# The ones beside the values, written by VectorE in place of ScalarE, in the opening of an attention and feed-forward block

**Chip, cores, metric.** One Trainium2 chip, one of its cores. The metric is device time in microseconds (us) of one execution; smaller is better.

## The reference, cut to what matters

A layer norm, attention of 32 heads of 16 features over 2048 positions, and a gated feed-forward layer, in bf16, with two residual additions:

```python
x = A_x                                            # 1 x 2048 x 512
h = x + attention(layernorm(x), A_wqkv, A_wo)      # 32 heads, head size 16, softmax over 2048 keys
n = layernorm(h)
return h + (sigmoid(n @ B_w_gate) * (n @ B_w_up)) @ B_w_down     # 512 -> 1792 -> 512
```

The softmax's sums come out of the same matmul as its weighted values: each head's 16 value columns have a 17th column of equal constants beside them. These are "the ones" (they hold 0.5). They are needed only when the first values are multiplied, after the first exponential.

## The kernel before: the parts concerned

`Vaug` holds the values: 128 partitions, 16 tiles x 32 heads x 17 columns of bf16. The ones are its last column: 512 elements in each partition, each 17 elements = 34 bytes from the next. The opening, in program order (each engine executes its own instructions in this order):

```python
Vaug = const.tile([P, NT, H, VW], BF16)            # NT=16, H=32, VW=17, DH=16
...
for i in range(TQ):                                # x tiles 0 to 3, two queues in turn
    load_x(0, i, 1, (nc.sync, nc.scalar)[i % 2])
...
nc.vector.memset(eps_t[:], 1e-5)
nc.scalar.activation(out=A0[:], in_=eps_t[:], func=ACT.Sqrt)     # loads the root's table early
fill = prep.tile([P, QC], BF16, name="fill")
nc.scalar.activation(out=Vaug[:, :, :, DH:VW], in_=eps_t[:].to_broadcast([P, NT * H]).rearrange(
    "p (t h o) -> p t h o", t=NT, o=1), func=ACT.Copy, scale=0.0, bias=0.5)      # the ones
nc.gpsimd.memset(fill[:], 1.0)                     # operand of TensorE's warming matmuls
nc.gpsimd.memset(eps4_t[:], 4e-5)
nc.gpsimd.memset(power[:], -0.5)
ramp = prep.tile([P, 2, 32], BF16, name="ramp")
for k in range(32):                                # 32 small memsets: 0, 1, ... 31
    nc.gpsimd.memset(ramp[:, 0, k:k + 1], float(k))
nc.gpsimd.tensor_scalar(out=eps4_t[:], in0=eps4_t[:], scalar1=1.0, scalar2=None, op0=ALU.mult)
...
nc.vector.memset(ident_bf[:], 0.0)
nc.vector.transpose(out=ramp[:, 1, :], in_=ramp[:, 0, :])        # waits for the ramp
for b in range(0, P, 32):                          # the identity: ramp == transposed ramp
    nc.vector.tensor_tensor(out=ident_bf[b:b + 32, b:b + 32], in0=ramp[b:b + 32, 0, :],
                            in1=ramp[b:b + 32, 1, :], op=ALU.is_equal)
...                                                # masks from the identity, on VectorE
```

Behind it the first layer norm runs from a fixed list. "As1" is the statistics of x tile 1 on ScalarE, "Ds0" those of tile 0 on VectorE, "Aq0" a root on ScalarE, "Dr0" a reciprocal and "Da0" a normalising on VectorE, "Pt0" a transposition on TensorE, "Pp10" a projection:

```python
START = "As1 Ds0 Ds2 Aq0 Dr0 Da0 Pt0 Aq2 Df1 Ds3 Aq1 Ae0 Pp10 Dr2 Da2 Aq3 Aexps ...".split()
```

So ScalarE reaches its statistics of tile 1 only after the ones, and VectorE takes two statistics (tiles 0 and 2) before the first reciprocal. TensorE executes matmuls on `fill` where it would be idle, so that its clock stays up.

## Time and profile before

| | before |
|---|---|
| device time, median of 3 runs | 732.0 us (731.65 to 732.0) |
| span of the profiled execution | 729.3 us |
| writing the ones (ScalarE, 512 elements per partition) | 2.36 us, from 3.04 us |
| VectorE's hole before the ramp's transpose | 1.45 us, 0.96 to 2.41 us |
| first reciprocal (VectorE) | 6.88 us |
| first transposition of a tile (TensorE) | 7.55 us |
| first exponential (ScalarE) | 12.68 us |

Positions are counted from the start of the profiled execution. The first exponential is the end of the opening: from there ScalarE is full to the end of the body. The lines of the profile behind the writing, the hole and the reciprocal are in the prediction. The one behind the first exponential, from the timeline (its columns are explained under the result), is:

```profile
12.68 3.77 ACT L1447 ACTIVATE pt<-PS 128x1024 f16<-128x1024 f32 x4 [0.50 <-PE PS L1067]
```

### The profile page before, as it was taken

What the parts mean: (1) busy time and instruction counts of PE and PEld (TensorE: products, weight loads), DVE (VectorE), ACT (ScalarE), POOL (GpSimd) and SP (SyncE); (2) the same over time, 40 slices, a digit from 0 to 9 for tenths busy, and PEclk for the clock granted to TensorE, in tenths of its full rate; (3) what the DMA queues carried; (4) which work ended last, traced back from release to release, by engine and by line L of the source; (5) the groups of instructions that cost most, each with busy time, mean ns of one, the idle gap of its engine ahead of it and who ended that gap; (6) DMA issues with size and microseconds to landing.
All of it is one profiled execution on the core that took longest, in us unless ns stands there. A gap on an engine that the chain in (4) does not pass through costs nothing.

```text
span 729.3 us, 26553 instructions
## 1 busy us (share of the span) xinstructions
PE 712.6 (98%) x11169; PEld 335.7 (46%) x11169; DVE 664.1 (91%) x1299; ACT 702.0 (96%) x787; POOL 426.4 (58%) x728
## 2 busy tenths in 40 slices
PE   8999999999999999999999999999999999999997
PEld 3322224444454445544545454545554455445564
DVE  7989989999999998999999999989999999999952
ACT  8999999999999999999999999999999999999962
POOL 2725657775566755656656766566664665666610
PEclk9999999999999999999999999999999999999999
DMA  8300006000223013211224023301322133013450
GB/s 259 88 11 10 11 8 178 2 3 2 74 78 95 14 33 105 85 45 46 67 62 109 9 82 89 75 17 44 106 67 60 39 103 103 10 24 89 117 161 19
DMA packets 85741, 47.39 MB, mean 65 GB/s; under 512 B 17520, under 2 KB 85616, under 8 KB 85616
## 3 DMA queue, kind: packets, MB, share of 16 engines
q1 hardware_dynamic: 85328, 45.37, 22.1%
q8 instruction: 89, 1.46, 0.9%
q14 instruction: 36, 0.29, 0.1%
q10 hardware_dynamic: 288, 0.26, 0.1%
HBM read 37.75 MB, written 2.10 MB: 55 GB/s over the span
## 4 chain that ended last, share of the span: by engine, by line
PE 69%; ACT 20%; DVE 7%; issue 2%; DMA 1%; POOL 1%; SPq 0%; ACTq 0%; DVEq 0%; POOLq 0%
PE PS L1067 23%; PE PS L1235 20%; ACT pt L1447 13%; PE PS L803 12%; PE PS L821 6%; DVE J L1259 3%; PE PS L321 3%; ACT xnT L1447 2%; PE PS L326 2%; PE PS L746 2%; ACT xb L1447 1%; ACT th L833 1%; ACT QTb L1447 1%; POOL J L1280 1%; DMA out_dram<-ob 1%
## 5 line engine op out<-in xcount | busy, mean ns | idle before, releaser
L1280 POOL INT64_ADD J<-J x658 | 407.9, 632 | 253.5 <-DVE J L1259 207.2
L1447 ACT ACTIVATE pt<-PS 128x1024 f16<-128x1024 f32 (+2 forms) x523 | 519.9, 1117 | 2.9 <-PE PS L1067 2.4
L1259 DVE TENSOR_SCALAR J<-PS 128x512 int16<-128x512 f32 x626 | 411.5, 678 | 17.7 <-PE PS L1067 12.6
L1067 PE MATMUL PS<-QT,KT 32*128 32x256 bf16 (+1 forms) x3712 | 264.1, 276 | 8.6 <-ACT pt L1447 3.6
L1235 PE MATMUL PS<-J,Vaug 128*17 128x256 f16 (+1 forms) x3195 | 226.1, 279 | 0.5 <-DVE J L1304 0.3
L1235 PE MATMUL PS<-pt,Vaug 128*17 128x256 f16 (+1 forms) x2042 | 198.3, 279 | 0.0
L1067 PEld LDWEIGHTS <-KT 32*128 32x128 bf16 x3840 | 89.7, 92 | 204.3 <-issue 200.5
L1235 PEld LDWEIGHTS <-Vaug 128*17 128x17 bf16 x5841 | 131.5, 90 | 78.4 <-issue 73.6
L803 PE MATMUL PS<-xnT,wgu 128*128 128x256 bf16 x784 | 112.9, 275 | 0.0
L1447 ACT ACTIVATE xnT<-PS 128x1024 f16<-128x1024 f32 (+1 forms) x85 | 92.2, 1116 | 0.5 <-PE PS L1067 0.2
L1304 DVE TENSOR_TENSOR J<-J 128x1024 f16<-128x1024 f16 (+1 forms) x110 | 78.4, 713 | 12.7 <-POOL J L1280 12.2
L803 PEld LDWEIGHTS <-wgu 128*128 128x128 bf16 x784 | 63.8, 98 | 38.5 <-issue 32.7
L821 PE MATMUL PS<-wd,hT 128*128 128x512 bf16 x196 | 56.7, 384 | 0.0
L833 ACT ACTIVATE th<-PS 128x512 f32<-128x512 f32 (+1 forms) x63 | 38.8, 616 | 8.8 <-DVE hT L816 5.0
L1235 PE MATMUL PS<-xnT,Vaug 128*17 128x256 f16 x346 | 46.7, 274 | 0.0
L1447 ACT ACTIVATE QTb<-PS 128x1024 f16<-128x1024 f32 x40 | 44.0, 1100 | 0.0
L875 DVE SCALAR_TENSOR_TENSOR hT<-th,PS 128x512 bf16<-128x512 f32 x49 | 33.1, 676 | 0.8 <-PE PS L803 0.8
L1134 DVE STREAM_TRANSPOSE xs<-PS 128x256 f32<-128x256 f32 (+1 forms) x60 | 27.5, 458 | 1.7 <-PE PS L1235 1.4
L1105 DVE TENSOR_TENSOR o<-xs,rsum 128x128 bf16<-128x128 f32 (+1 forms) x60 | 24.5, 409 | 2.1
L1447 ACT ACTIVATE xb<-PS 128x1024 f16<-128x1024 f32 (+1 forms) x25 | 26.0, 1086 | 0.3 <-issue 0.2
L1235 PE MATMUL PS<-QTb,Vaug 128*17 128x256 f16 x160 | 25.7, 274 | 0.0
L1447 ACT ACTIVATE pe<-PS 128x1024 f16<-128x1024 f32 (+1 forms) x21 | 21.9, 1094 | 0.9 <-PE PS L1067 0.8
(126 smaller groups left out, 390.7 us busy)
## 6 DMA issues: line engine op xcount, KB each, us to landing
wgu<-in_B_w_gate_dram SPq DMA_DIRECT2D x49, 256.0 KB, 3.0
wgu<-in_B_w_up_dram SPq DMA_DIRECT2D x49, 256.0 KB, 3.4
out_dram<-ob SPq DMA_DIRECT2D x16, 128.0 KB, 1.7
QT<-qd SPq DMA_DIRECT2D x112, 16.0 KB, 1.8
wd<-in_B_w_down_dram SPq DMA_DIRECT2D x1, 1792.0 KB, 9.2
xr<-in_A_x_dram SPq DMA_DIRECT2D x14, 128.0 KB, 3.4
xb<-in_A_x_dram SPq DMA_DIRECT2D x6, 256.0 KB, 5.5
J<-in_B_w_gate_dram SPq DMA_DIRECT2D x4, 384.0 KB, 4.3
```

The costliest lines, as they stand in the source:

```text
L803: nc.tensor.matmul(ps[:, 0:PARTS[r][2]].rearrange("p (i q) -> p i q", q=P), lhsT=w[:, d, :], rhs=hn_of(r)[:, :, d, :], start=(d == 0), sto ...
L821: nc.tensor.matmul(ps, lhsT=hT[:, f, i * P:(i + 1) * P], rhs=wd[:, f, :], start=(f == 0), stop=(f == FC - 1))
L833: nc.scalar.activation(out=th[:, 0:ps.shape[-1]], in_=ps, func=ACT.Tanh, scale=0.5)
L875: nc.vector.scalar_tensor_tensor(out=hT[:, f:f + k, 0:w], in0=th[f][:].rearrange("p (k n) -> p k n", k=k), scalar=1.0, in1=ps2.rearrange(" ...
L1067: nc.tensor.matmul(pss[:, ui, i * CW[qc]:(i + 1) * CW[qc]], lhsT=KT[g // 2][32 * j:32 * j + 32, k * P:(k + 1) * P], rhs=q[32 * j:32 * j + ...
L1105: nc.vector.tensor_tensor(out=o2[:, 0:w // 32, DH * a:DH * a + DH], in0=xs[:, 0:w // 32, 0:DH], in1=rec.to_broadcast([P, w // 32, DH]), op ...
L1134: j = dve(650 - ns[0], lambda: nc.vector.transpose(out=xs[:, 0:w // 32, :].rearrange("p b r -> p (b r)"), in_=src), LAST, st["xs"], pr=-1)
L1235: nc.tensor.matmul(dst[32 * j:32 * j + VW, 0:w], lhsT=un.v[:, kt * SPAN[qc] + i, h, :], rhs=un.ap[:, i * w:(i + 1) * w], start=clears and ...
L1259: nc.vector.tensor_scalar(out=J[:, 0, k, :], in0=src, scalar1=ZOFF, scalar2=float(-min(CHORDS)), op0=ALU.add, op1=ALU.max)
L1280: nc.gpsimd.int64_add(words(s), words(0), CHORDS[s - 1] * (1 + 2 ** 16 + 2 ** 32 + 2 ** 48))
L1304: nc.vector.tensor_tensor(out=f1, in0=f1, in1=J[:, 0, 0:k, :].bitcast(FP16), op=ALU.add)
L1447: ex = nc.scalar.activation(out=pt, in_=pss[:, 0:wa, :], func=ACT.Exp, scale=AS)
```

## The change

Intent: VectorE waits 1.45 us for the ramp anyway. Let it write the ones there, "in single-rate mode", and so take 2.36 us from ScalarE, which is on the path to the first exponential.

```diff
     fill = prep.tile([P, QC], BF16, name="fill")
-    nc.scalar.activation(out=Vaug[:, :, :, DH:VW], in_=eps_t[:].to_broadcast([P, NT * H]).rearrange(
-        "p (t h o) -> p t h o", t=NT, o=1), func=ACT.Copy, scale=0.0, bias=0.5)
     nc.gpsimd.memset(fill[:], 1.0)
...
     nc.vector.memset(ident_bf[:], 0.0)
+    nc.vector.tensor_scalar(out=Vaug[:, :, :, DH:VW], in0=eps_t[:].to_broadcast([P, NT * H]).rearrange(
+        "p (t h o) -> p t h o", t=NT, o=1), scalar1=0.0, scalar2=0.5, op0=ALU.mult, op1=ALU.add)
     nc.vector.transpose(out=ramp[:, 1, :], in_=ramp[:, 0, :])
```

Nothing else changes its place on any engine.

## The prediction

> **What bounds the kernel now.** I read the page of the kernel before from the top: busy times, then the slices, then the chain that ended last.
>
> ```profile
> span 729.3 us, 26553 instructions
> PE 712.6 (98%) x11169; PEld 335.7 (46%) x11169; DVE 664.1 (91%) x1299; ACT 702.0 (96%) x787; POOL 426.4 (58%) x728
> PE 69%; ACT 20%; DVE 7%; issue 2%; DMA 1%; POOL 1%; SPq 0%; ACTq 0%; DVEq 0%; POOLq 0%
> ```
>
> TensorE and ScalarE are both busy nearly to the end, and the page's slices show no hole anywhere. In the body, from 13 us to about 697 us, ScalarE runs its exponentials end to end (the busy table by stretch gives 17.00 of 17.00 us from 13 to 30 us and 239.27 of 240.00 us from 240 to 480 us). So a microsecond saved before the first exponential moves the whole body earlier by about a microsecond, unless a later wait swallows it. A microsecond is 0.14% of the span, so the question is not whether 2% is reached but how much of the opening shrinks. Therefore I went to the opening: the first 13 us in the timeline of single instructions, and the chain of work that ended last over the same stretch.
>
> The chain, in order of time (start, length, what):
>
> ```profile
> 1.64 1.28 ACT L251
> 2.92 0.01 issue
> 2.93 0.20 ACT warm L251
> 3.13 2.26 ACT Vaug L253
> 5.40 0.52 ACT junk L364 x2
> 5.92 0.02 issue
> 5.94 0.72 ACT junk L366 x2
> 6.66 0.19 ACT QT L381
> 6.86 0.02 issue
> 6.88 0.17 DVE QT L418
> ```
>
> The instruction that the change removes, the writing of the ones (L253), is on the chain with 2.26 us. Behind it on ScalarE stand the statistics of x tile 1 (L364, L366) and the first square root (L381), and VectorE waits 1.40 us for that root before its reciprocal (L418), on which the normalising, transposing and projecting of the first tiles depend.
>
> VectorE's rows in the same timeline show the hole that the change wants to use:
>
> ```profile
> 0.80 0.06 DVE L250 MEMSET eps_t<- 128x1 f32 x1 [0.80 <-PEq L1665]
> 0.85 0.11 DVE L265 MEMSET ident_bf<- 128x64 uint32 x1
> 2.41 0.21 DVE L266 STREAM_TRANSPOSE ramp<-ramp 128x32 bf16<-128x32 bf16 x1 [1.45 <-POOL ramp L260]
> 2.65 0.70 DVE L268 TENSOR_TENSOR ident_bf<-ramp 32x32 bf16<-32x32 bf16 x4
> 3.39 0.29 DVE L272 TENSOR_REDUCE mask<-ident_bf 128x2 f32<-128x128 bf16 x1
> 3.71 0.17 DVE L274 TENSOR_SCALAR maskz<-mask 128x2 f32<-128x2 f32 x1
> 3.79 0.69 DVE L281 BATCH_NORM_STATS2 st<-xb 128x6 f32<-128x512 bf16 x1
> ```
>
> The hole is 1.45 us long, from 0.96 to 2.41 us, and ends when GpSimd has written the ramp (32 small memsets, 1.25 to 2.37 us). From 2.41 us to 5.48 us VectorE has no hole at all, so whatever sticks out beyond 2.41 us delays everything after it on VectorE one for one.
>
> **What the Trainium skill says.** "ScalarE: Activation LUTs", section "What ACT_TABLE_LOAD costs", gives an ACTIVATE with immediate scale and bias 186 ns + 0.833 ns per element: 186 + 512 x 0.833 = 612 ns. The trace agrees for the zeroing of an accumulator from the same broadcast source (L430, 128x512, contiguous, into PSUM: 607 ns) and disagrees with L253 (2357 ns). Source and count are the same; what differs is the destination, single bf16 elements 17 elements (34 bytes) apart in SBUF. "SBUF — State Buffer", section "Door 1: The DMA port swizzle", names a reason: SBUF has 16-byte cachelines and an access that crosses to a new line pays. That fits the extra (2357 - 607) / 512 = 3.4 ns per element, though this trace alone does not show it. "Vector Engine (DVE) Microarchitecture Reference", section 5.2 "Measured stream behaviour on trn2", has the same for VectorE: a destination that steps 24 words at each element ran at 2.50 ns per element instead of 1.05. "Advanced Engine Details and Errata", section "VectorE Performance Modes", says that a two-port mode takes SBUF source and destination with even outer counts, and that its second port is shared with GpSimd, so that the two block each other. The trace has a two-port rate at fp32 in its tail (L1623, 128x512: 419 ns, against 678 ns for the PSUM-sourced L1259), and the same-shaped normalising at L791 ranges from 514 to 828 ns beside a busy GpSimd, which would fit such blocking.
>
> **The change part by part.**
>
> Removed: one ACTIVATE of ScalarE, 2.36 us in its row, 2.26 us of it on the chain. Not all comes back, because the statistics need x tile 1. That tile's load is issued at 0.73 us and lands 2.8 us later, at 3.5 us. They can then start at about 3.55 us. The two passes take 0.54 + 0.18 + 0.03 + 0.72 = 1.47 us, where 0.54 us is the gap from L366 to its accumulator read, taken for both passes since the first was held back by L253's tail. They end at 5.02 us, the root 0.19 us later at 5.21 us, in place of 6.86 us: 1.65 us earlier. Now VectorE is the later one: the statistics of tile 2 occupy it until 5.48 us, and the reciprocal starts at about 5.39 us (back-to-back instructions overlap by some 0.09 us) in place of 6.88 us: 1.49 us earlier. The normalised tile 0 is then ready at about 6.0 us in place of 7.5 us.
>
> The next limit is TensorE's static order: 13 warming matmuls run from 1.31 to 6.44 us whatever happens. The first transpose comes after them, at 6.35 to 6.45 us in place of 7.55 us: 1.1 to 1.2 us earlier. From there each step has room: the first copy of a transposed tile on ScalarE ends at about 7.4 us (8.57), after four more warming matmuls the first projection starts at about 7.5 us (8.65); its weights, issued at 1.67 us with 4.35 us to land, are there at 6.05 us, the others at 6.55 us. On ScalarE the fourth root follows the copy, then the exponential's table load, at about 7.6 us (8.93). On VectorE the remaining normalising keeps its 1.49 us. The last transpose, copy and projection before the first scores come out 1.1 to 1.3 us earlier, and so does the first exponential, 12.68 us before. The value weights are issued at 3.80 us and take 5.7 us, so 9.5 us is early enough for their first use, now near 12.2 us.
>
> Added: one tensor-scalar of VectorE on 512 strided elements. The instruction order of the two builds confirms that it stands between the zeroing of the identity and the ramp's transpose, that the other engines keep their orders, and that no engine gets a new wait for it; it only waits for VectorE's own first memset. It can start at 0.98 us. Its length is the open term. In single-rate mode without a stride penalty it would take about 0.68 us (as the other 512-element single-rate instructions here); with the skill's strided 2.50 ns per element, an estimate, 512 x 2.50 = 1.28 us plus about 0.1 us fixed = 1.4 us, ending at 2.4 us, just inside the hole; with ScalarE's own per-element cost, 4.24 ns, 2.2 to 2.3 us, ending at 3.25 us.
>
> Nothing else moves: the body's work is the same in kind, count and order.
>
> Sum: about 1.2 us if the new instruction fits its hole, less what it sticks out. I weigh a fit at 55%, and give the others a mean gain of 0.65 us: 0.55 x 1.2 + 0.45 x 0.65 = 0.95 us. From the 732.0 us median, that is 731.05 us; the three runs spread from 731.65 to 732.0 us with a mean of 731.9 us, and taking half of that difference into account I put the point at 731.0 us.
>
> **The rivals.**
>
> (1) The strided write is as slow on VectorE as on ScalarE. It then ends at about 3.25 us, the ramp's transpose is 0.85 us late, the statistics of tiles 0 and 2 end at 6.3 us instead of 5.48 us, and the reciprocal starts there: only 0.55 to 0.65 us earlier than before. For it: the 2357 ns of L253, whose extra lies in the destination. Against it: the skill's smaller VectorE figure. Time about 731.4 us.
>
> (2) The instruction is taken in a two-port mode after all (fp32 source and bf16 destination both in SBUF, all counts even) and blocks GpSimd's ramp memsets, which lie exactly in its interval. The ramp would then be ready up to the instruction's length, 0.4 to 0.9 us, later, with the same consequence as in (1): about 731.3 us. Against it stands the intent that the change states, single-rate.
>
> (3) The gain of the opening is lost again in the body: another phase of VectorE, GpSimd and TensorE against each other, or a weight load that comes no earlier. For it: the body has small waits (ScalarE waited 2.4 us in all for scores, VectorE 12.6 us for them). Against it: the order on every engine is fixed, ScalarE's body is full, and all later loads are issued by the same flow, so they shift with it. It would give 731.5 to 732.2 us.
>
> (4) A better phase, or a further saving because ScalarE no longer contends with anything in the opening: 730.3 us at best.
>
> **How the range and chances follow.** A full gain of 1.2 us with a favourable phase gives 730.2 us, a full loss of the gain 731.9 to 732.0 us; nothing in the opening can cost more than the 0.9 us by which the new instruction could overrun, and that is more than repaid by the 1.49 us freed. So 730.2 to 731.9 us should hold eight times in ten. Two per cent is 14.6 us; the whole opening to the first exponential is 12.7 us long, so neither side of 2% is within reach: 0.01 each.
>
> **What would show it.** In the changed profile: the first pass of the statistics (L364 before) starts near 3.55 us, not 4.93; the first root ends near 5.2 us; the first reciprocal starts near 5.4 us, with little idle time ahead of it; the first transpose starts at 6.35 to 6.45 us, right behind the warming matmuls; the first exponential at about 11.45 us. The new VectorE row should last 0.7 to 1.4 us and the ramp's transpose stay at 2.41 us. The prediction is wrong in its sizes if that row is longer than 1.5 us or the ramp comes later, and wrong in its mechanism if the first exponential comes a microsecond earlier and the span does not.

## The result, and the profile after

| | before | after |
|---|---|---|
| first measurement: median of 4 and 4 runs | 731.83 us | 731.99 us |
| later, 11 and 5 runs on another occasion | 731.85 us | 731.63 us |
| ratio after/before, first measurement | | 1.0, interval 0.9983 to 1.0017 |
| ratio after/before, later | | 0.9997, interval 0.9985 to 1.001 |
| first reciprocal, first and later trace | 6.88 us | 6.31, 6.43 us |
| first exponential, first and later trace | 12.68 us | 12.06, 12.19 us |

A ratio is the mean time of one kernel's fast runs over that of the other's of the same rounds, so not quite the ratio of the medians quoted. All outputs are right. The time stayed the same: the means differ by 0.00 us in the first measurement and by 0.11 us in the later one. The first median lies 0.09 us above the predicted range, the later one inside it. The intervals are wide beside this: the later one still allows the kernel after to be 1.1 us faster or 0.7 us slower. So the times by themselves cannot tell a gain of half a microsecond from none; what follows rests on positions in the traces.

Yet the profile shows a shorter opening. Here is the timeline of the kernel after (start, length, engine, line, instruction, destination and source, and in brackets the idle time before it and what ended it):

```profile
0.90 2.60 DVE L264 TENSOR_SCALAR Vaug<-eps_t 128x512 bf16<-128x512 f32 x1
1.25 1.12 POOL L258 MEMSET ramp<- 128x1 bf16 x32
3.13 0.37 DVE L266 STREAM_TRANSPOSE ramp<-ramp 128x32 bf16<-128x32 bf16 x1
3.32 0.63 ACT L364 ACTIVATE junk<-xb 128x512 bf16<-128x512 bf16 x1 [0.18 <-DMA xb<-in_A_x_dram]
5.63 0.30 ACT L381 ACTIVATE QT<-QT,eps_t 128x1 f32<-128x1 f32 x1 [0.84 <-DVE QT L284]
12.06 2.86 ACT L1447 ACTIVATE pt<-PS 128x1024 f16<-128x1024 f32 x3 [0.50 <-PE PS L1067]
```

ScalarE's statistics (L364) start at 3.32 us, as soon as x is there, instead of at 4.93 us. But the new VectorE instruction lasts 2.60 us, not the 1.45 us of its hole. The ramp is complete at 2.37 us as before, and its transpose ends at 3.13 + 0.37 = 3.50 us instead of 2.41 + 0.21 = 2.62 us. So VectorE is 0.88 us late, and ScalarE's root (L381) now waits 0.84 us for VectorE's statistics. The chain that ended last, over the same stretch of the kernel after, has changed its engine:

```profile
0.96 2.54 DVE Vaug L264
3.50 0.04 DVE ramp L266
...
6.21 0.18 DVE QT L284
6.39 0.06 DVE QT L418
```

Before, ScalarE stood here from 1.64 to 6.86 us. Now VectorE does, from the ones to the reciprocal without a hole. The gain of the opening is 0.5 to 0.6 us in place of the 1.2 us of a fit.

**In the traces the rest was lost in the body.** I numbered the exponentials from the last backward and compared the start of each with that in the first trace of before. Negative is earlier (us):

| at (us) | before, second trace | after | after, second trace |
|---|---|---|---|
| 14 to 40 | 0.00 | -0.61 | -0.48 |
| 44 | 0.00 | -0.31 | -0.18 |
| 240 | +0.02 | -0.28 | -0.11 |
| 276 | +0.14 | +0.09 | +0.34 |
| 580 | +0.13 | +0.09 | +0.37 |
| 612 to 696 | +0.12 | +0.86 | +0.39 |

There are three places. Near 43 us, ScalarE's wait before one exponential grows. This is the table of waits of ScalarE from 40 to 50 us (in total, times, longest), before and then after:

```profile
ACT xb L1447 <- issue: 0.2, 1, 0.2
```

```profile
ACT xb L1447 <- issue: 0.5, 1, 0.5
```

The same 0.3 us is lost there in every trace that starts early (eight of them, 0.30 to 0.38 us), and not in one that starts late (see e_act_twice). So something there does not come earlier with the rest, but "issue" means that the profile names no releaser, and I have not found one. Near 260 us another 0.4 us goes, of which the second trace of the unchanged kernel loses 0.12 us as well. The trace of e_bench, whose body is that of the kernel before, loses 0.51 us between 240 and 276 us, so a loss of this size there needs no change in the opening; its cause is not settled. Near 608 us the first trace of after loses 0.69 us and its second trace nothing. This is the timeline of the first trace there:

```profile
606.67 1.12 DVE L1304 TENSOR_TENSOR J<-J 128x1024 f16<-128x1024 f16 x1 [0.21 <-POOL J L1280]
608.31 0.43 DVE L1134 STREAM_TRANSPOSE xs<-PS 128x256 f32<-128x256 f32 x1
608.79 0.27 PE L1235 MATMUL PS<-J,Vaug 128*17 128x256 f16 x1 [0.58 <-DVE xs L1134]
```

VectorE's addition L1304 takes 1.12 us (0.69 us before, at the same place) beside GpSimd's additions, the transposing of results behind it comes at 608.31 instead of 607.44 us, and TensorE waits 0.58 us for it. As the second trace of the same kernel has no such wait, and e_quarter's trace loses 0.68 us at the same place although it is the fastest kernel, this is a matter of phase and not a cost of the change. With it the profiled span of after is 1.0 us longer than that of before, while the means are equal: one span says little about half a microsecond.

### The profile page after: what moved, and what is told of

Its sections match the earlier page's. It is cut to its first block, busy times and chain, and to the rows that moved or that the text cites. A ratio compares the mean times of both kernels' runs of the same rounds, so it can differ in the third digit from the quotient of the medians.

```text
span 730.3 us, 26553 instructions
## 1 busy us (share of the span) xinstructions
PE 713.4 (98%) x11169; PEld 336.2 (46%) x11169; DVE 666.7 (91%) x1300; ACT 700.6 (96%) x786; POOL 426.8 (58%) x728
## 4 chain that ended last, share of the span: by engine, by line
PE 66%; ACT 19%; DVE 9%; issue 3%; POOL 1%; DMA 1%; SPq 0%; DVEq 0%; POOLq 0%; ACTq 0%
PE PS L1067 22%; PE PS L1235 19%; ACT pt L1447 14%; PE PS L803 11%; PE PS L821 6%; DVE J L1259 4%; PE PS L321 3%; ACT xnT L1447 2%; PE PS L326 2%; PE PS L746 2%; ACT xb L1447 1%; POOL J L1280 1%; ACT th L833 1%; ACT QTb L1447 1%; PE PS L1641 1%
## 5 line engine op out<-in xcount | busy, mean ns | idle before, releaser
L1304 DVE TENSOR_TENSOR J<-J 128x1024 f16<-128x1024 f16 (+1 forms) x110 | 78.8, 716 | 13.5 <-POOL J L1280 12.9
```

The lines of the kernel that those rows point to most:

```text
L1304: nc.vector.tensor_tensor(out=f1, in0=f1, in1=J[:, 0, 0:k, :].bitcast(FP16), op=ALU.add)
```

## The experiments

**Theories.** *Port theory*: the tensor-scalar is not single-rate. It runs in a mode that takes both of VectorE's ports, one of which GpSimd uses too. Alone it would fit the hole; beside GpSimd's memsets, which occupy the same 1.45 us, one of the two must wait. *Stride rival*: the write itself is that slow, because of its 34-byte step, and GpSimd has no part in it. *Body rival*: the opening does not matter, because the body gives back whatever is won. The quoted expectations name theories by letters: the port theory is D and the stride rival is E (there E also includes that any strided write of VectorE stands in GpSimd's way); A, B and C are explained where they first stand.

### The unchanged kernel after, once more

> The changed kernel again, for the spread from run to run. In the first profile the first exponential came 0.62 us earlier (12.06 for 12.68 us), and the gain was lost in three places of the body (near 43 to 48 us, 264 to 273 us and 606 us). Theory A (the losses are waits that depend on the phase of VectorE, GpSimd and the loads against each other, and partly chance): the first exponential is again at 12.06 us, within 0.1 us, the losses near 606 us are not all there again, and the time is within 0.6 us of the kernel before. Rival B (a lasting cost of the change eats exactly the gain): the same three losses, each within 0.05 us, again. Rival C (the gain is real and the first four runs hid it): 0.6 us faster in the mean of the rounds.

Measured on chip 0, five rounds: 731.79, 732.38, 731.53, 731.63, 731.35 us; ratio 0.9997, the same. Its trace answers the question of the port better than any other. Timeline of this second trace of after:

```profile
0.90 1.48 DVE L264 TENSOR_SCALAR Vaug<-eps_t 128x512 bf16<-128x512 f32 x1
1.19 1.23 POOL L254 MEMSET eps_t<- 128x1 f32 x1
1.25 2.14 POOL L258 MEMSET ramp<- 128x1 bf16 x32
3.43 0.21 DVE L266 STREAM_TRANSPOSE ramp<-ramp 128x32 bf16<-128x32 bf16 x1 [1.05 <-POOL ramp L258]
```

In the first trace VectorE needed 2.60 us and GpSimd's ramp 1.12 us. Here VectorE needs 1.48 us and the ramp 2.14 us. GpSimd's memset ahead of the ramp (L254, 0.10 us in the first trace) lasts 1.23 us and ends at 2.42 us, just after VectorE's end at 2.38 us. The instruction streams are the same, and the other engine loses. Either way the ramp's transpose ends about 0.9 to 1.0 us late (3.50 and 3.64 us). The stride rival, in which GpSimd has no part, cannot make the ramp 1.02 us longer.

### The ones on GpSimd, behind the ramp

```diff
     for k in range(32):
         nc.gpsimd.memset(ramp[:, 0, k:k + 1], float(k))
+    nc.gpsimd.memset(Vaug[:, :, :, DH:VW], 0.5)
...
-    nc.vector.tensor_scalar(out=Vaug[:, :, :, DH:VW], ...)
```

> The ones are written by GpSimd, right behind its ramp, so that they are on no chain of the opening. Expected for the opening, as in the prediction with a fitting instruction: first pass of the statistics at about 3.3 us, first reciprocal at about 5.4 us, first exponential at about 11.4 us, so 1.2 us before the kernel before and 0.6 us before the changed one. If the first reciprocal still starts near 6.3 us, VectorE's late ramp was not what held the changed kernel. For the total: rival C (an earlier start is kept one for one) says 1.2 us faster, 730.6 us; theory A (waits of the body take most of it) says between 0 and 0.8 us faster. GpSimd's memset itself: 0.5 us if a strided destination costs it nothing (its contiguous 512 elements took 0.52 us), 2 to 3 us if it pays as VectorE and ScalarE did.

Measured on chip 0: 729.89, 730.8, 730.67, 737.84, 730.69, 731.07 us, median 730.75. The run of 737.84 us had a granted clock of 0.991 but counted as fast, so the ratio is 1.0004 with a wide interval (0.9975 to 1.0033); without it the mean is 730.62 us against 731.85 us. Timeline:

```profile
2.31 2.27 POOL L259 MEMSET Vaug<- 128x512 bf16 x1
3.72 0.89 DVE L273 TENSOR_SCALAR maskz<-mask 128x2 f32<-128x2 f32 x1
```

With VectorE's list as before, the ramp's transpose is back at 2.41 us, the first reciprocal comes at 5.55 us and the first exponential at 11.32 us. The gain that the prediction named for a fit exists. GpSimd's memset now runs beside VectorE's 2-element tensor-scalar L273, and that lasts 0.89 us instead of 0.17 us, up to 4.61 us, just after the memset's end at 4.58 us. The transpose (0.21 us), the comparisons (0.71 us) and the reduction (0.29 us) ahead of it run beside the same memset without loss, so it isn't every instruction of VectorE that waits. The meeting of the two engines has moved, not gone.

### Half on VectorE, half on GpSimd

```diff
+    nc.gpsimd.memset(Vaug[:, NT // 2:NT, :, DH:VW], 0.5)          # behind the ramp
...
-    nc.vector.tensor_scalar(out=Vaug[:, :, :, DH:VW], in0=eps_t[:].to_broadcast([P, NT * H])...
+    nc.vector.tensor_scalar(out=Vaug[:, 0:NT // 2, :, DH:VW], in0=eps_t[:].to_broadcast([P, NT * H // 2])...
```

> VectorE writes the first 256 ones, GpSimd the other 256. If VectorE's 2.60 us are a cost per element (4.9 ns each), its half takes 1.3 to 1.4 us, ends at 2.3 us, within the hole, and the ramp's transpose is back at 2.41 us; the first exponential is then as early as in the kernel with GpSimd alone, about 11.4 us. If it is a fixed cost of the instruction (a first use, a wait for a port while GpSimd writes its memsets), it takes over 2 us still. Total as for the kernel with GpSimd alone.

Measured on chip 0: 730.96, 730.49, 730.66, 730.22, 730.47 us; ratio 0.998 (0.9967 to 0.9993). Timeline:

```profile
0.89 0.94 DVE L265 TENSOR_SCALAR Vaug<-eps_t 128x256 bf16<-128x256 f32 x1
1.25 1.59 POOL L258 MEMSET ramp<- 128x1 bf16 x32
```

Here both lose: the ramp takes 1.59 instead of 1.12 us, though VectorE is done at 1.83 us. The transpose is 0.47 us late, the first reciprocal comes at 5.88 us and the first exponential at 11.64 us.

### The ones written twice by ScalarE

The kernel before with its activation L253 duplicated.

> The kernel before with the ones written twice by ScalarE, so with the opening made longer on its chain by 1.9 to 2.3 us. First exponential at about 14.6 to 15.0 us in place of 12.68 us. Rival C (what the opening gains or loses is kept one for one): 733.7 to 734.2 us. Theory A (the body's waits absorb part): clearly less than 1.9 us longer, 0.5 to 1.5 us. The profile shows at which places of the body the shift grows or shrinks: if near 43 to 48 us and 264 to 273 us, these are the places where a wait not tied to the opening resets the phase.

Measured on chip 0: 735.92, 735.31, 735.89, 737.54, 735.81 us; ratio 1.0058 (1.0045 to 1.0071). The first reciprocal came 2.40 us later (9.28 us), as one more activation should make it, but the first exponential came 4.38 us later (17.05 us). The busy table by stretch (stretch; its length; busy time and count of PE, PEld, DVE, ACT, POOL; granted clock; DMA share; GB/s) of this kernel, and then of the kernel before for the second stretch, shows why:

```profile
6.00:10.00 4.00, 0.44 (x3) 0.06 (x2) 0.65 (x4) 3.40 (x7) 0.00 (x0) 0.88 1.06 346
10.00:14.00 4.00, 4.00 (x27) 2.90 (x28) 3.21 (x11) 2.56 (x5) 0.26 (x1) 0.50 1.09 348
```

```profile
10.00:14.00 4.00, 4.00 (x44) 2.29 (x41) 3.43 (x10) 3.30 (x7) 0.26 (x1) 1.00 1.03 336
```

TensorE ran out of warming matmuls and stood idle for 3.56 us before its first transposition. From 10 to 14 us its granted clock was 0.50, where before had 1.00. This is as the Trainium skill has it, "TensorE: Matmul & The Clock Gate", section "Part 1: The HAM clock gate": the clock falls to half after an idle window of about 3.4 us. The warming matmuls are sized to the opening, so a change that made the opening 2.4 us longer cost about 2 us more on top.

The 4.38 us are 4.85 us at the last exponential: a later start is passed on in full. That alone does not refute the body rival, since an earlier start could still be lost. The trace of e_pool does: its first exponential is 1.35 us earlier than in before, and its last 1.38 us. What holds is weaker, that an earlier start can lose some tenths.

### A memset on VectorE, meant as a single-port write

```diff
-    nc.vector.tensor_scalar(out=Vaug[:, :, :, DH:VW], ...)
+    nc.vector.memset(Vaug[:, :, :, DH:VW], 0.5)
```

> VectorE writes the same strided ones in the same place, but by a memset, which has no source. In the kernel after, VectorE's tensor-scalar and GpSimd's memsets hold each other up: in the first profile VectorE's took 2.60 us and GpSimd's ramp ended at 2.4 us, in the second 1.48 us and the ramp ended at 3.4 us, and with half the elements 0.94 us and 2.9 us. Theory D (the tensor-scalar runs in a two-port mode and shares a port with GpSimd): the memset leaves GpSimd alone, its ramp ends at 2.4 us, the ramp's transpose starts at 2.41 us unless the memset itself is longer than 1.45 us; the first exponential comes 1.2 to 1.35 us before the kernel before, 11.35 to 11.5 us, and the total 0.6 to 1.3 us earlier. Rival E (any strided write of VectorE stands in GpSimd's way, or costs over 2 us for itself): the ramp's transpose starts at 2.9 us or later, first exponential 11.7 to 12.2 us.

Measured on chip 15: 730.72, 731.44, 730.59, 731.53, 731.03 us; ratio 0.9995 (0.9982 to 1.0008). Timeline:

```profile
2.65 0.48 DVE L264 MEMSET Vaug<- 128x512 bf16 x1 [1.70 <-issue]
2.78 0.38 DVE L265 STREAM_TRANSPOSE ramp<-ramp 128x32 bf16<-128x32 bf16 x1
```

Read carelessly, this is a memset of 0.48 us. But it has nothing to wait for, and its predecessor ended at 0.96 us: it occupies VectorE up to 3.13 us, about 2.2 us, and the "issue" in front of it is its own work. GpSimd's ramp keeps its 1.12 us beside it, as the port theory wants. And the write takes over 2 us by itself, as the stride rival wants. The transpose ends 0.54 us late (3.16 us), the first reciprocal comes at 5.95 us and the first exponential at 11.71 us. So a write at this slower rate doesn't fit the hole either.

### The ones on GpSimd, repeated on another chip

The kernel of e_pool unchanged.

> The kernel with the ones on GpSimd again, since one of its six times was an outlier (737.84 us beside 729.89 to 731.07 us). First exponential at 11.3 us again; if the outlier was the chip's and not the kernel's, five runs at 729.9 to 731.1 us, a ratio of 0.998 to 0.999; if the kernel has a second state of its own, again one of about six near 738 us.

Measured on chip 15: 731.42, 731.14, 731.74, 731.95, 730.76 us, and one slow run of 742.04 us left out; ratio 0.9998 (0.9985 to 1.0011). The first exponential comes at 11.32 us again, yet the gain of 1.35 us falls to 0.52 us between 14 and 25 us. GpSimd's first instruction behind the load of its library comes at 15.21 us in this trace (14.27 us in e_pool, 11.55 us in before, 10.94 us in after). The 2.28 us memset stands ahead of that load, and the late load costs most of what the opening won: from 12 to 26 us TensorE waits 0.6 us for GpSimd's normalised tiles, which it doesn't do in e_pool. I therefore do not count this version as better.

### The unchanged kernel before, once more

> The kernel before profiled once more, as the measure of what the body does by itself. If the steps of 0.2 to 0.7 us in the shift between two profiles (near 43, 256 to 276, 590 and 608 us) are chance, they stand between two profiles of this one kernel too: first exponential at 12.68 us within 0.1 us in both, and the ends apart by up to 1 us. If the two profiles agree within 0.1 us all along, the steps between before and after belong to the change.

One run, 731.08 us. Up to 262 us its exponentials agree with those of the first trace within 0.02 us; by 276 us they are 0.13 us late, and 0.10 us at the end. So differences of a tenth in the table above are within what two traces of one kernel show, and the 0.3 us at 43 us are not (0.12 us, in the trace of e_bench, is the most that a kernel with the old opening loses there).

### The write alone, with different steps

At the end of the kernel before, 512-element writes of 0.5 to bf16 with growing distance of the elements, one after another on each engine (GpSimd idle during VectorE's, but ScalarE's and GpSimd's overlapping from 729.5 us on); durations in ns from single instructions of the trace:

```python
def steps(x, k, n=512):
    return x[:, 0:n * k].rearrange("p (n k) -> p n k", k=k)[:, :, 0]
for k in (1, 2, 4, 8, 16, 17):
    nc.vector.tensor_scalar(out=steps(fv2, k), in0=one, scalar1=0.0, scalar2=0.5, op0=ALU.mult, op1=ALU.add)
...                       # the same as memset, as nc.scalar.activation, as nc.gpsimd.memset
```

> The kernel before with isolated writes of 512 bf16 elements at its end, when no other engine works on them: on VectorE by tensor-scalar with the destination's step 1, 2, 4, 8, 16 and 17 elements, by memset with step 1 and 17, and 256 fp32 elements with step 1 and 17; on ScalarE the ACTIVATE with the same steps; on GpSimd memsets with step 1, 2, 8, 17. If the cost is the line that each element falls on, step 8 and above cost about the same, and step 1 to 4 little; if it is the odd half-word, 17 costs more than 16, and fp32 at step 17 costs nothing extra. For VectorE: step 1 at 0.42 us[...] says two-port mode, 0.68 us single-rate; step 17 alone, with GpSimd idle, below 1.3 us says that over half of the 2.60 us in the changed kernel was waiting for GpSimd, over 2 us that it was the stride. ScalarE: step 17 at 2.36 us as in the kernel before, step 1 at 0.61 us. The output is right; the time is a few us over that of the kernel before.

| step (elements) | 16-byte lines touched | VectorE tensor-scalar | ScalarE activation | GpSimd memset |
|---|---|---|---|---|
| 1 | 64 | 415 | 620 | 525 |
| 2 | 128 | 456 | 771 | 666 |
| 4 | 256 | 737 | 1343 | |
| 8 | 512 | 1309 | 2472 | 2390 |
| 16 | 512 | 1302 | 2378 | |
| 17 | 512 | 1252 | 2366 | 2261 |

The time grows with the lines touched and stops growing when every element has its own line, from 8 elements = 16 bytes on. Per line beyond the first few, ScalarE takes (2472 - 1343) / 256 = 4.4 ns, GpSimd (2390 - 666) / 384 = 4.5 ns, and VectorE's tensor-scalar (1309 - 737) / 256 = 2.2 ns: half. That is what two ports in place of one would make of it. The strided memset of VectorE shows its trap again; timeline of this kernel, step 1 and then step 17:

```profile
726.60 0.48 DVE L1657 MEMSET Vaug<- 128x512 bf16 x1 [0.17 <-DVE Vaug L1656]
728.90 0.48 DVE L1658 MEMSET Vaug<- 128x512 bf16 x1 [1.82 <-issue]
```

Rows of equal length, but the second has 1.82 us of its work in front of it: about 2.3 us, the single-port figure. One thing stays open: 256 fp32 elements 17 elements apart took only 393 ns (285 ns side by side), where bf16 on as many lines (512 elements, two to a line) took 737 ns. Whether half-word writes pay extra was not tested.

### The two engines beside each other, alone

Also at the end of the kernel before: GpSimd's 32 small memsets (1) alone, (2) beside the strided tensor-scalar with its source in SBUF, (3) the same with its source in PSUM, (4) the tensor-scalar alone, each started by a small activation.

> The kernel before with four short tests at its end, each started by one small ACTIVATE: (1) GpSimd's 32 one-element memsets alone, (2) the same beside VectorE's tensor-scalar on 512 bf16 elements 34 bytes apart with its source in SBUF, as in the change, (3) the same with the source in PSUM, (4) the tensor-scalar from SBUF alone. Theory D (two-port mode, a port shared with GpSimd): 1.25 us in (4); in (2) either the tensor-scalar is 0.9 to 1.4 us longer or the memsets end 0.9 to 1.4 us later than in (1); in (3) the tensor-scalar takes 2.2 to 2.4 us (512 lines at 4.4 ns on one port), and the memsets are as fast as in (1), 1.1 us. Rival E (any strided writing of VectorE disturbs GpSimd): the memsets are late in (3) as well.

Timeline:

```profile
725.58 0.98 POOL L1655 MEMSET QT<- 128x1 f32 x32 [29.09 <-ACT QT L1657]
...
726.88 2.10 DVE L1663 TENSOR_SCALAR Vaug<-QT 128x512 bf16<-128x512 f32 x1 [7.10 <-ACT QT L1657]
726.90 0.98 POOL L1655 MEMSET QT<- 128x1 f32 x32 [0.34 <-ACT QT L1657]
...
729.62 2.32 DVE L1668 TENSOR_SCALAR Vaug<-PS 128x512 bf16<-128x512 f32 x1 [0.64 <-ACT PS L1667]
...
732.05 1.25 DVE L1672 TENSOR_SCALAR Vaug<-QT 128x512 bf16<-128x512 f32 x1
```

Alone the tensor-scalar takes 1.25 us and would have fitted the 1.45 us. Beside 0.98 us of GpSimd memsets it takes 2.10 us: 0.85 us more, nearly all of GpSimd's time. With a source in PSUM, which by the conditions of the Trainium skill ("Advanced Engine Details and Errata", section "VectorE Performance Modes") leaves no two-port mode, it takes 2.32 us, near the 2.2 to 2.3 us of the strided memset, and GpSimd is done a microsecond before it. The port theory holds, with one blemish: in case 3 GpSimd's memsets paused once, taking 1.24 us from first to last, and I expected them as fast as alone (0.98 us). That a strided write of VectorE disturbs GpSimd in any mode is still unlikely: in e_memset the ramp kept its 1.12 us beside one.

### A quarter on VectorE, the rest on GpSimd behind its library

The conclusion put to use: VectorE takes only what fits beside the ramp, and GpSimd's part stands behind its library load, where it has time, so that it delays nothing.

```diff
     nc.gpsimd.tensor_scalar(out=eps4_t[:], in0=eps4_t[:], scalar1=1.0, scalar2=None, op0=ALU.mult)
+    nc.gpsimd.memset(Vaug[:, NT // 4:NT, :, DH:VW], 0.5)
...
-    nc.vector.tensor_scalar(out=Vaug[:, :, :, DH:VW], in0=eps_t[:].to_broadcast([P, NT * H])...
+    nc.vector.tensor_scalar(out=Vaug[:, 0:NT // 4, :, DH:VW], in0=eps_t[:].to_broadcast([P, NT * H // 4])...
```

> A version meant to beat the others: VectorE writes the first 128 ones (the first four tiles of values) in its hole, GpSimd the other 384 after its library has been loaded, where neither the ramp nor the load is held up. VectorE's part 0.4 to 0.7 us; the ramp's transpose at 2.5 to 2.7 us; first reciprocal at 5.5 to 5.7 us; first exponential at 11.3 to 11.5 us, 1.2 to 1.35 us before the kernel before. GpSimd's part about 1.8 us from some 10.5 to 13 us on. If the shift lives on in the body as in the other early kernels (0.3 us lost near 43 us, 0.2 to 0.4 us near 265 us): total 0.4 to 0.9 us earlier; against it, GpSimd's first normalising at about 14 us may wait for the memset, which would cost up to 0.9 us by 25 us.

Measured on chip 14: 730.83, 729.65, 730.34, 730.12, 729.91 us, median 730.12 against 731.52 us; ratio 0.9978 (0.9965 to 0.9992). Timeline:

```profile
0.90 0.65 DVE L265 TENSOR_SCALAR Vaug<-eps_t 128x128 bf16<-128x128 f32 x1
2.60 0.21 DVE L267 STREAM_TRANSPOSE ramp<-ramp 128x32 bf16<-128x32 bf16 x1 [1.05 <-POOL ramp L258]
10.93 1.72 POOL L260 MEMSET Vaug<- 128x384 bf16 x1
```

The ramp is only 0.19 us late, the first reciprocal comes at 5.59 us and the first exponential at 11.35 us. GpSimd's 1.72 us end at 12.65 us, and its next instruction waits 1.38 us for VectorE, so they cost nothing. This is the fastest version measured, by 1.5 us in the mean against before; its interval and that of the plain change (0.9985 to 1.001, on another chip) overlap a little.

### Half and half, repeated on the same chip

The kernel of e_half unchanged.

> The half-and-half kernel on another chip, since it was the only one whose interval lay clear of the kernel before (0.998, 0.9967 to 0.9993). If that was the kernel's own: again 0.997 to 0.999 and first exponential at 11.64 us. If it was the chip or the run: 0.9985 to 1.0005.

Measured on chip 14: 730.51, 731.77, 729.62, 730.42, 731.28 us; ratio 0.9989 (0.9975 to 1.0003), first exponential at 11.63 us, as before. It lies between the plain change and the quarter, as its ramp does.

## Why the prediction was right or wrong

The prediction that the time would stay the same was right. This was nearly certain and tests little: 2% is 14.6 us, and the whole opening lasts 12.7 us. Its point was not reached: the measured mean gain is about 0.1 us and not 0.95 us, though the later interval alone doesn't exclude 0.95 us. By the sign that it set for itself it was wrong in its sizes: the new row is longer than 1.5 us in one trace (2.60 us; 1.48 us in the other), and the transpose starts at 3.13 and 3.43 us instead of 2.41 us.

One table holds the argument. "Late" is how much later than 2.62 us the ramp's transpose ends, "gain" is before's mean time minus this kernel's. The recorded intervals leave each gain uncertain by 0.9 to 1.2 us, so the argument rests on the other columns:

| kernel | late | first reciprocal | 5.39 + late | first exponential | exponential minus reciprocal | gain (us) |
|---|---|---|---|---|---|---|
| e_quarter | 0.19 | 5.59 | 5.58 | 11.35 | 5.76 | 1.50 |
| e_half | 0.47 | 5.88 | 5.86 | 11.64 | 5.76 | 1.29, 0.95 |
| e_memset | 0.54 | 5.95 | 5.93 | 11.71 | 5.76 | 0.55 |
| after | 0.88 | 6.31 | 6.27 | 12.06 | 5.75 | 0.00 |
| after, second trace | 1.02 | 6.43 | 6.41 | 12.19 | 5.76 | 0.11 |
| before | 0 | 6.88 (held by ScalarE) | | 12.68 | 5.79 | |

- **What ScalarE gives up: right.** Its statistics start at 3.32 us (predicted 3.55 us), and VectorE becomes the later one. The reciprocal would come at 5.39 us if the ramp were on time: in every other kernel of the table it comes at 5.39 us plus the ramp's lateness, within 0.04 us. (e_pool is not in the table: its ramp is on time, but its reciprocal comes 0.16 us later than 5.39 us, because of the wait of L273.) "Whatever sticks out beyond 2.41 us delays everything after it on VectorE one for one" is thereby shown.
- **The length of the new instruction: the term that was mis-sized.** The prediction gave a fit 55%, at 1.4 us. Alone it takes 1.25 us, even less. But it does not run alone. Rival (2), the two-port mode that blocks the ramp's memsets, is what happened in the second trace; in the first one GpSimd blocked VectorE, which the rival had not foreseen. The delay is at or above the upper end of its "0.4 to 0.9 us" either way (0.88 and 1.02 us). Against it I had set the change's own words, "single-rate". A word in a change is not a measurement: by the skill's conditions that I cited there, source, destination and counts all allow the two-port mode. The size of rival (1), 2.2 to 2.3 us for a one-port write, was right too (2.32 us with the source in PSUM, about 2.2 us for the memset).
- **The gain of a fit: mis-sized, too small.** I let the warming matmuls set the first transposition at 6.35 us at the earliest, and got 1.2 us. In e_pool the first transposition came only at 6.69 us and the exponential still at 11.32 us; in all these kernels the exponential follows the first reciprocal by 5.75 to 5.79 us. The later normalisings on VectorE hold it, not the first transposition: the chain that ended last, in e_quarter and in after, stays on VectorE up to the end of the third normalising (8.28 and 8.99 us). Nor do the warming matmuls run to 6.44 us "whatever happens": they end at 5.87 to 7.04 us in the traces. For a full fit that makes 5.39 + 5.76 = 11.15 us, an estimate: 1.5 us of gain.
- **The gain of a misfit: right.** I assumed 0.65 us; the two traces show 0.61 and 0.48 us at the first exponential.
- **Rival (3), the loss in the body: right in kind, underweighted.** The point took no loss there. All early traces lose 0.30 to 0.38 us near 43 us, and most some tenths near 260 us. In the two traces of after, starts 0.61 and 0.48 us earlier have become 0.86 and 0.40 us later at the last exponential; the times are too coarse to size the mean loss. What causes the first of these losses stays open.
- **A misreading without effect.** The prediction puts the first use of the value weights near 12.2 us; in the trace of before it is at 13.4 us.
- **The range** of 0.9 us below 731.9 was drawn for a gain that would be kept in part. With one of two medians 0.09 us outside, its upper end was too tight for four runs that spread over 1.1 us.

## What to carry to other kernels

An idle hole of one engine isn't free if the instruction put there shares a port with what the other engine does in that hole: ask not only whether it fits, but what its neighbour is doing meanwhile, and measure it beside that neighbour. When a write is dear because each element lands in a line of its own, splitting it between engines, with each part where that engine truly waits, gave more in the mean (1.5 us) than moving it whole to VectorE (0.1 us), though the two intervals overlap a little. When the saving is under a microsecond in 730, look at positions in the trace of two executions, not at one span.

## What the Trainium skill lacked or had wrong

- "SBUF — State Buffer", section "Door 1: The DMA port swizzle": it says that crossing to a new 16-byte line costs, but gives no size. The runs show 4.4 to 4.5 ns per line for bf16 writes of ScalarE and GpSimd, and 2.2 ns for VectorE's tensor-scalar.
- "Vector Engine (DVE) Microarchitecture Reference", section 5.2 "Measured stream behaviour on trn2": its 2.50 ns per element is for 4-byte words. Here a bf16 write from a PSUM source took 2.32 us / 512 = 4.5 ns per element, and fp32 from a source in SBUF 393 ns / 256 = 1.5 ns. An estimate for bf16 from the page's figure comes out wrong for one port (1.4 us against 2.32 us).
- "Advanced Engine Details and Errata", section "VectorE Performance Modes": it says that the two engines block each other, which the runs confirm, but not how much it costs. Which one waits is treated on another page, "SBUF — State Buffer", so that is not lacking. The runs show both outcomes for one kernel, although its rows start in the same order each time (VectorE's at 0.90 us, GpSimd's next memset at 1.19 us): VectorE 2.60 us instead of 1.25 us with GpSimd undisturbed, or GpSimd's ramp 2.14 us instead of 1.12 us with VectorE at 1.48 us.
- No page has it ("PSUM — Partial Sum Buffer" only hints that a memset's own row is no measure of its time): the row of a VectorE memset of 512 elements shows 0.48 us at steps 1 and 17 alike, and at step 17 the rest of its work (1.70 and 1.82 us) appears as idle time "issue" ahead of it.
- "GPSIMD Engine Reference", section "2.1 Instruction dispatch": it gives one length, about 6 us, for the load behind which GpSimd's first instruction waits, and no spread. In the thirteen traces that instruction came 7.9 to 10.9 us after the MODIFY_POOL_CONFIG ahead of it, at 10.26 to 15.21 us, and the latest case cost 0.84 us.
